# Linear attention with a mixture of experts on one core: q and k loaded as long contiguous runs into a wider tile, with three unit buffers in place of four

## The chip, the cores and the metric

The kernel runs on 1 core of one Trainium2 chip. The metric is the device time of one execution in microseconds (us); lower is better. Before the change three runs took 681.4, 684.25 and 685.61 us, median 684.25.

## What is computed

The reference, cut to what matters. Inputs q, k and v have shape (8, 8, 576, 64): batch, heads, sequence, head size d. All is float32.

```python
def phi(x):
    proj = np.einsum('bhsd,df->bhsf', x, w_phi)          # w_phi: 64 x 128
    proj = proj - np.max(np.abs(proj), axis=-1, keepdims=True)
    return np.concatenate([np.exp(proj), np.exp(-proj)], axis=-1)
q_p, k_p = phi(q), phi(k)
kv = np.einsum('bhsf,bhsd->bhfd', k_p, v)
z = np.sum(k_p, axis=2)
num = np.einsum('bhsf,bhfd->bhsd', q_p, kv)
den = np.einsum('bhsf,bhf->bhs', q_p, z)[..., None] + 1e-06
x = num / den                                            # to rows (token, 512)
# tokens with x @ w_skip > 0: out = x + gate * relu(x @ w1[e]) @ w2[e], e = argmax(x @ w_gate)
# all other tokens: out = x
```

## The kernel before, in words

The program has two stages. The first, attention, works in **units**: one unit is four heads of one batch of either k or q, so 16 units of k and 16 of q. The four heads are two pairs (`pr`). The 576 tokens of a head are 32 runs of 18 tokens; one run of 18 tokens of 64 numbers is 4608 contiguous bytes of the input.

- `st_load` (L250) brings a unit into the tile `u.raw` of shape 128 x 2 x 18 x 32. A partition stands for (half of d, head of the pair, run): the lower 64 partitions hold d from 0 to 31, the upper 64 hold d from 32 to 63. It issues four DMAs, one for each pair and half of d, all on SyncE's queue (line L256). The row of one token is cut in two halves, so each piece that a DMA moves is 32 numbers, 128 bytes. The tile has four buffers, shared by k and q in turn.
- `st_t` (L276) turns the loaded rows with VectorE: L289 transposes the last two of the 18 tokens of both pairs (the tail, step i = 0), L291 the first 16 tokens of one pair (steps i = 1 and 3). After the i = 3 transpose a unit's `raw` buffer is free. ScalarE rounds the result to `hi` (L292), and GpSimd or VectorE forms `lo` = x - `hi` (L294). These come from the pool `hl`.
- `st_proj` multiplies `hi` and `lo` by `wph` and `wpl`, the two parts of w_phi (TensorE, L306 to L308), takes the largest absolute value (VectorE, `m`, L312) and subtracts it (VectorE, `u`, L321).
- `st_exp_k` and `st_exp_q` take the exponentials (ScalarE), and for k form the sums `z` (GpSimd, L353). `st_use_k` makes k'v (L388, L395), `st_use_q` q'(kv) (L486), `norm` divides (VectorE, L437 to L449). `post` finds each token's expert and stores the rows.

A loop over steps t runs the stages of all units as a pipeline with the lags `CFG["lag"]`; the q units follow the k units of the same index by six steps, and one unit takes five steps. At a unit's step i = 0 the load of the next unit of its kind is emitted. v is loaded at L265 and L274 (`v` and its tails `vt`), also on SyncE's queue, as are the stores of rows (L503, L505, L564, L566) and of results (L630, L635). Each engine, and SyncE's queue, runs its instructions in the order in which they stand. TensorE's order is the written one from step 8 to step 79; elsewhere, and on all other engines, a scheduler orders them when the program is built. A DMA into a buffer waits on SyncE until the last reader of the buffer's former content has run.

The second stage, the experts, loads weight chunks (`wraw_c`, L184 and L187), splits them in two parts (L188, L189) and runs the two layers in slots of up to 256 tokens.

Of the kernel before, what the change touches and what calls it, by code (L numbers as in the profile page):

```python
# [18 lines left out]
P = 128  # L19
SLOT = 256  # L20
CFG = {'ql': -2, 'q1': 0, 'vtl': 3, 'at': 6, 'cp': 0, 'ini': 'vvpvppvvpvp', 'inz': '', 'lo': {('E', 0): 'pppvpppp', ('E', 1): 'pppppppp'}, 'lod': 'vppvvvpv', 'seq': ('E', 'E', 'C', 'C', 'SC', 'D', 'DS', 'C', 'C', 'D'), 'pre': (2,), 'rows': (1, 2), 'rxg': (0,) * 6, 'lag': (1, 3, 4, 5, 6), 'post': (4, 5, 7), 'hook': (-1, -1, -1), 'man': (8, 79), 'dnow': 0, 'off': 6, 'order': 'EPAZUT', 'direct': (), 'nb': {'K': 1, 'P': 3, 'U': 2, 'O': 2}, 'apools': (('ld', 2), ('hl', 5), ('up', 5), ('zp', 2), ('ep', 7), ('kvp', 6), ('xp', 2)), 'mpools': (('rawp', 1), ('mx', 2), ('mo', 2), ('wseta', 1), ('wsetb', 1))}


@with_exitstack
def kernel(
# [26 lines left out]
    NA1 = NAUG - 1  # L52
    # a row of xrows: the token, its gate, its number
    XW = DM + 2
    EB = B - 3
    NTE = 9 * (EB // 2) + 9
    # slots: full ones, ones of up to 192 tokens, ones of up to 128
    NSD = (NTOK + E * 63) // SLOT
# [22 lines left out]
    nc.scalar.activation(out=warm, in_=warm, func=AF.Exp)  # L81
    # w_phi in the rows of either head of a pair, and which rows are whose
    wsrc = const.tile([P, NF], F32, name="wsrc")
# [22 lines left out]
    iota_p = const.tile([P, P], F32, name="iota_p")  # L106
    # the tails of a quad's v, each pair in its own rows, zeros in the other's
    vts = [const.tile([P, 2, 2, D], F32, name="vt%d" % j) for j in range(2)]
# [14 lines left out]
    pad0 = const.tile([P, 2, 2], I32, name="pad0")  # L123
    # of every slot: the rows to gather and the rows to scatter to
    ft = const.tile([P, NSL, 4], I32, name="ft")
# [84 lines left out]
    def places(g, pad, v):  # L210
        # v is 0 in an empty place, else 1 + the row to gather; what to add so that no row is scattered from an empty one
        nc.vector.tensor_scalar(out=g, in0=v, scalar1=-1.0, scalar2=0.0, op0=ALU.add, op1=ALU.max)
        nc.vector.tensor_scalar(out=pad, in0=v, scalar1=0.0, scalar2=BIG, op0=ALU.is_equal, op1=ALU.mult)

    early = []
    # ------------------------------------------------------------------ attention
    with ExitStack() as actx:
        pools = {}
        for nm, bufs in CFG["apools"]:
            pools[nm] = actx.enter_context(tc.tile_pool(name=nm, bufs=bufs))  # L220
        ld, hl, zp, up, ep, kvp, xp = (pools[nm] for nm in ("ld", "hl", "zp", "up", "ep", "kvp", "xp"))

        # a head is 32 runs of 18 tokens; partition (half of d, head of the pair, run)
        kv_in = {
            "k": k.rearrange("b h s d -> (b h s d)").rearrange("(u r p t c) -> u r p t c", r=2, p=64, t=18, c=D),
            "q": q.rearrange("b h s d -> (b h s d)").rearrange("(u r p t c) -> u r p t c", r=2, p=64, t=18, c=D),
        }
        vv = v.rearrange("b h s d -> (b h s d)").rearrange("(u h p t c) -> u p h t c", h=4, p=32, t=18, c=D)
        outv = out.rearrange("(b p j) m -> b p j m", p=32, j=18)
        # rows of xrows: two batches after each other, then the tails of both  # L230
        xr = xrows.rearrange("(b x) m -> b x m", x=2 * S)
# [19 lines left out]
        def st_load(u):  # L251
            src = kv_in[u.kind]
            u.raw = ld.tile([P, 2, 18, 32], F32, tag="raw", name="raw", bufs=4)
            for pr in range(2):
                for dh in range(2):
                    nc.sync.dma_start(  # L256
                        out=u.raw[dh * 64:dh * 64 + 64, pr],
                        in_=src[u.g, pr][:, :, dh * 32:dh * 32 + 32],
                    )

# [15 lines left out]
        def st_t(u, i):  # L276
            if i == 0:
                n, sfx = P, "t"
                src = u.raw[:, :, 16:18, :].rearrange("p r t c -> p r (t c)")
            elif i in (1, 3):  # L280
                n, sfx = 4 * P, ""
                src = u.raw[:, i // 2, 0:16, :].rearrange("p (q g) c -> p q g c", g=4)
            else:
                return
            xT = hl.tile([P, n], F32, tag="xT" + sfx, name="xT" + sfx, bufs=2)
            hi = hl.tile([P, n], F32R, tag="hi" + sfx, name="hi" + sfx)
            lo = hl.tile([P, n], F32R, tag="lo" + sfx, name="lo" + sfx)
            if i == 0:
                nc.vector.transpose(out=xT.rearrange("p (r c) -> p r c", r=2), in_=src)  # L289
            else:  # L290
                nc.vector.transpose(out=xT.rearrange("p (g q c) -> p q g c", g=4, q=4), in_=src)  # L291
            nc.scalar.activation(out=hi, in_=xT, func=AF.Copy)  # L292
            nlo[0] += 1
            (nc.vector if CFG["ini"][nlo[0] - 1:nlo[0]] == "v" else nc.gpsimd).tensor_tensor(  # L294
                out=lo, in0=xT, in1=hi.bitcast(F32), op=ALU.subtract)
            u.hlp[(i + 1) // 2] = (hi, lo)
# [136 lines left out]
        def norm(o, xdst, ldst, shape):  # L433
            # o: [P, 4, NAUG]
            den = small.tile([P, 4], F32, tag="den", name="den")
# [16 lines left out]
        def st_use_q(u, i):  # L452
# [5 lines left out]
            if i == 0:  # L458
                # the tails of two batches side by side
                for h in range(4):  # L460
# [52 lines left out]
        def post(b):  # L513
# [40 lines left out]
            )  # L554
            # the gate goes with the token's row
            nc.vector.tensor_reduce(out=ss[:, 0:nt], in_=ex[:, 0:nt], axis=AX.X, op=ALU.add)
# [20 lines left out]
            def rank():  # L577
                # rank of each computed token among those of its expert
                r = bank("O")[:, 0:nt * E]
# [66 lines left out]
        def pick(j):  # L646
            # the expert with the most tokens so far: its first tokens make a slot of their own, done early;
            # the ranks of its later tokens start anew
            cn = bank("O")[:, 0:E]
# [105 lines left out]

    # ------------------------------------------------------------------ experts
    pools = {}
# [31 lines left out]
    def hidden_c(hv):  # L789
        # 192 tokens: the last 64 with both their parts next to each other  # L790
        hh = mo.tile([P, 2, SLOT], F32R, tag="hh", name="hh", bufs=5)
# [8 lines left out]
    def half1(ws, xs):  # L800
        # a slot of 128 tokens: the tokens' columns stay, the weights stream
        _, xh, xl, _, _ = xs
# [38 lines left out]
    def store_c(y, xs):  # L841
        xg, to = xs[0], xs[3]
        # the sums of the high and of the low parts of 64 tokens lie in either half of y
        g, x, r = xg[1][:, DM:DM + 1], xg[1][:, 0:DM], slice(0, 64)
# [10 lines left out]
    def mm1(ws, xs, hooks=()):  # L855
# [3 lines left out]
        for c, (wh, wl) in enumerate(ws):  # L859
            if n < SLOT:  # L860
                # fewer than 256 columns take as long as 256: the products with both parts of x side by side
                hsum = mo.tile([P, 2, n], F32, tag="hsum", name="hsum")
# [65 lines left out]

    # the slots of the tokens that are left: per expert full ones of 256, a rest of up to 192 or of up to 128 in
    # one of its own kind  # L930
    eid = const.tile([1, NSL], I32, name="eid")
# [4 lines left out]
    def tables():  # L936
# [23 lines left out]
        nc.vector.tensor_tensor(out=exc, in0=inc, in1=nn, op=ALU.subtract)  # L960
        # a token's column: its rank, in groups of 128, plus cf[0] where it is below cf[1], else plus cf[2]
        nc.vector.tensor_scalar(out=cf[:, 0], in0=exc[:, 0], scalar1=2.0, scalar2=1.0, op0=ALU.mult, op1=ALU.add)
# [6 lines left out]
        nc.vector.tensor_tensor(out=cf[:, 2], in0=cf[:, 2], in1=cf[:, 1], op=ALU.subtract)  # L969
        # the experts of the slots, and how many there are  # L970
        le = const.tile([1, NSL, E], F32, name="le")
# [6 lines left out]
        nc.vector.tensor_scalar(out=eid[:, 0:NSL], in0=ef, scalar1=float(E - 1), scalar2=None, op0=ALU.min)  # L978
        # the column of each token
        rk = const.tile([P, NT], F32, name="rk")  # L980
# [44 lines left out]
        places(ft[:, NS2:NSL, 0:1], ft[:, NS2:NSL, 2:3], ix[:, 2 * NS2:NCOL].rearrange("p (t s) -> p t s", s=1))  # L1025
        # the slots that the sequence below leaves
        ov = const.tile([1, 8], F32, name="ov")
# [6 lines left out]
        for c, to, left in ((0, 0, "DC"), (1, 3, "CS")):  # L1034
# [100 lines left out]
```

## Time and profile before

| what | value |
|---|---|
| runs | 681.4, 684.25, 685.61 us |
| profiled execution, its own time | 681.4 us |
| span of the profiled execution | 681.4 us |
| TensorE (PE) busy | 600.5 us, 88% |
| VectorE (DVE) busy | 539.6 us, 79% |
| GpSimd (POOL) busy | 440.7 us, 65% |
| ScalarE (ACT) busy | 373.7 us, 55% |
| DMA packets | 221684, of them 160293 under 512 B; 108.17 MB |
| raw loads | 64 for k and 64 for q, 144 KB each |
| mean granted TensorE clock | 0.974 |

A row of the chain or of a group names engine, line and operation, then what it writes `<-` what it reads. "x64" is a count. In rows of waits, the engine at the left stood idle until the one at the right had finished; the numbers are the total in us, the count and the longest. In rows of windows come, for each stretch of the span, the busy time of each engine with its number of instructions, the granted TensorE clock, the busy share of the 16 DMA engines and the rate that they moved. SPq is the queue of SyncE: a row there is the time that it takes to issue DMAs.

### The profile page before, as it was taken

How to read it: one execution, taken by the hardware profiler on the slowest of the kernel's cores; microseconds unless marked ns; L12 is line 12 of the kernel's file. 1: busy time of each engine (PE TensorE's matmuls, PEld its weight loads, DVE VectorE, ACT ScalarE, POOL GpSimd, SP SyncE). 2: the span in 40 equal slices, each digit the busy share in tenths (PEclk: the TensorE clock that was granted, in tenths of full speed). 3: DMA queues.
4: the chain of work that ended last, by engine and by line, in shares of the span. 5: the costliest groups of instructions: out<-in, count | busy, mean ns of one | idle time of the engine just before them, and what ended most of it. 6: DMA issues, size and time to landing. Idle time of an engine off the chain costs nothing. (4 is left out here: it accounts for less than half of the span.)

```text
span 681.4 us, 16258 instructions
## 1 busy us (share of the span) xinstructions
PE 600.5 (88%) x6045; PEld 514.2 (75%) x6045; DVE 539.6 (79%) x1216; ACT 373.7 (55%) x747; POOL 440.7 (65%) x383
## 2 busy tenths in 40 slices
PE   4897999979998889999899991999999989979994
PEld 3585888768877778877788881888878879868893
DVE  6868888887978978978998799679988876677830
ACT  4566665647565475656564533147757556555510
POOL 6886777777777596868774458276575485374411
PEclk9898999999999999999999996899989999999998
DMA  9898664857675667655316387269788877774500
GB/s 130 127 145 157 112 168 91 160 108 133 144 144 90 146 117 133 142 103 114 105 33 195 114 222 232 72 203 296 249 262 268 268 238 267 251 238 139 192 17 27
DMA packets 221684, 108.17 MB, mean 159 GB/s; under 512 B 160293, under 2 KB 202405, under 8 KB 221604
## 3 DMA queue, kind: packets, MB, share of 16 engines
q1 hardware_dynamic: 218272, 97.60, 58.8%
q0 software_dynamic: 3200, 9.45, 4.0%
q8 instruction: 49, 0.80, 0.5%
q14 instruction: 31, 0.25, 0.1%
q10 hardware_dynamic: 132, 0.07, 0.0%
HBM read 83.86 MB, written 24.02 MB: 158 GB/s over the span
## 5 line engine op out<-in xcount | busy, mean ns | idle before, releaser
L189 POOL TENSOR_TENSOR w<-wraw_c,w 128x1024 fp32r<-128x1024 f32 x45 | 109.9, 2454 | 70.6 <-ACT w L188 64.3
L188 ACT ACTIVATE w<-wraw_c 128x1024 fp32r<-128x1024 f32 x96 | 101.0, 1057 | 56.9 <-DMA wraw_c<-in_moe_w_dram 44.9
L353 POOL TENSOR_TENSOR z<-ek 128x512 f32<-128x512 f32 x64 | 81.7, 1277 | 54.9 <-ACT ek L345 45.1
L312 DVE TENSOR_REDUCE m<-ps_P 128x4 f32<-128x512 f32 (+1 forms) x160 | 96.4, 620 | 3.7 <-PE ps_P L308 3.6
L321 DVE TENSOR_TENSOR u<-ps_P,m 128x512 f32<-128x512 f32 (+1 forms) x160 | 95.9, 621 | 0.4
L306 PE MATMUL ps_P<-wph,hi 128*128 128x256 f32 x256 | 80.8, 316 | 16.6 <-ACT hi L292 8.5
L486 PEld LDWEIGHTS ps_O<-kva,eq 128*64 128x64 f32 x2048 | 75.2, 137 | 18.0 <-ACT eqt L373 7.3
L189 DVE TENSOR_TENSOR w<-wraw_c,w 128x1024 fp32r<-128x1024 f32 x51 | 75.4, 1481 | 14.6 <-ACT w L188 14.5
L486 PE MATMUL ps_O<-kva,eq 128*64 128x74 f32 x2048 | 78.4, 229 | 5.0 <-ACT eqt L373 3.2
L294 POOL TENSOR_TENSOR lo<-xT,hi 128x512 fp32r<-128x512 f32 x61 | 78.1, 1280 | 5.0 <-ACT hi L292 4.8
L308 PE MATMUL ps_P<-wph,lo 128*128 128x256 f32 x256 | 73.4, 287 | 0.0
L307 PE MATMUL ps_P<-wpl,hi 128*128 128x256 f32 x256 | 73.2, 286 | 0.0
L388 PE MATMUL ps_K<-ek,v 128*64 128x256 f32 x512 | 71.3, 396 | 1.5 <-DMA v<-in_v_dram 1.5
L372 ACT ACTIVATE eq<-ps_U 128x512 f32<-128x512 f32 x64 | 37.9, 593 | 57.2 <-PE ps_U L366 49.2
L306 PEld LDWEIGHTS ps_P<-wph,hi 128*128 128x128 f32 x256 | 49.4, 193 | 20.4 <-ACT hi L292 9.0
L908 PE MATMUL ps_O<-w,hh 128*128 128x512 f32 x160 | 62.4, 400 | 1.4 <-DVE hh L796 1.3
L836 POOL DMA_INDIRECT out_dram<-o,si x17 | 22.2, 1305 | 54.1 <-DVE o L834 44.4
L913 PE MATMUL ps_O<-w,hlo 128*128 128x512 f32 x120 | 49.0, 410 | 5.1 <-DVE hlo L796 5.1
L307 PEld LDWEIGHTS ps_P<-wpl,hi 128*128 128x128 f32 x256 | 49.7, 194 | 0.0
L308 PEld LDWEIGHTS ps_P<-wph,lo 128*128 128x128 f32 x256 | 49.6, 194 | 0.2 <-DVE lo L294 0.2
L366 PE MATMUL ps_U<-ident,u 128*128 128x128 f32 x288 | 48.4, 286 | 0.6 <-DVE u L321 0.6
L289 DVE STREAM_TRANSPOSE xTt<-raw 128x128 f32<-128x128 f32 x32 | 9.9, 309 | 48.8 <-DMA raw<-in_k_dram 26.8
(233 smaller groups left out, 1570.9 us busy)
## 6 DMA issues: line engine op xcount, KB each, us to landing
wraw_c<-in_moe_w_dram SPq DMA_DIRECT2D x96, 512.0 KB, 4.6
raw<-in_k_dram SPq DMA_DIRECT2D x64, 144.0 KB, 4.0
raw<-in_q_dram SPq DMA_DIRECT2D x64, 144.0 KB, 4.1
v<-in_v_dram SPq DMA_DIRECT2D x64, 128.0 KB, 3.7
out_dram<-xm SPq DMA_DIRECT2D x32, 256.0 KB, 4.4
xrows<-xm SPq DMA_DIRECT2D x8, 516.0 KB, 4.2
xrows<-xm SPq DMA_DIRECT2D x8, 512.0 KB, 4.7
vt<-in_v_dram SPq DMA_DIRECT2D x64, 16.0 KB, 2.6
```

The costliest lines, as they stand in the source:

```text
L188: nc.scalar.activation(out=hi, in_=raw, func=AF.Copy)
L189: (eng or nc.vector).tensor_tensor(out=lo, in0=raw, in1=hi.bitcast(F32), op=ALU.subtract)
L294: (nc.vector if CFG["ini"][nlo[0] - 1:nlo[0]] == "v" else nc.gpsimd).tensor_tensor(out=lo, in0=xT, in1=hi.bitcast(F32), op=ALU.subtract)
L306: nc.tensor.matmul(o, hi[:, c], wph, start=True, stop=False)
L307: nc.tensor.matmul(o, hi[:, c], wpl, start=False, stop=False)
L308: nc.tensor.matmul(o, lo[:, c], wph, start=False, stop=True)
L312: nc.vector.tensor_reduce(out=m[:, 0:nt], in_=pv, axis=AX.X, op=ALU.max, apply_absolute_value=True)
L321: nc.vector.tensor_tensor(out=uu[:, 0:nt, :], in0=pv, in1=m[:, 0:nt].rearrange("p (t o) -> p t o", o=1).broadcast_to([P, nt, NF]), op=ALU. ...
L353: zeng.tensor_tensor(out=z, in0=e[:, 0:2, :], in1=e[:, 2:4, :], op=ALU.add)
L388: nc.tensor.matmul(o[hd * 64:hd * 64 + 64, :], u.v[:, 2 * pr + hd, g * D:(g + 1) * D], u.e[i][:, 2 * j + hd, :], start=(g == 0), stop=False,)
L486: nc.tensor.matmul(ov[s * 64:s * 64 + 64, 2 * j + hd, :], e[:, half, j, hd, s * 64:s * 64 + 64], kva[:, half, 2 * pr + hd, :], start=(half ...
L908: nc.tensor.matmul(y[sub], hh[:, t], wh[:, fi, :], start=first, stop=False)
```

## The change

`st_load` issues two DMAs for a unit in place of four, one for each half of d. Each takes, for every run of 18 tokens, 4480 contiguous bytes (1120 numbers): the run without its last 32 numbers. For the upper half of d it starts 128 bytes later. So in either half of the partitions the numbers that are wanted stand at the first 32 places of each 64, and the other 32 of each token are loaded and not read. The tile is 128 x 2 x 18 x 64, twice as large, and has three buffers. `st_t` reads the first 32 places of each token. The pool `hl` has four buffers of `hi` and `lo` in place of five. Comments are gone; nothing else differs in the source.

```diff
-CFG = {..., 'apools': (('ld', 2), ('hl', 5), ...
+CFG = {..., 'apools': (('ld', 2), ('hl', 4), ...
...
         def st_load(u):
-            src = kv_in[u.kind]
-            u.raw = ld.tile([P, 2, 18, 32], F32, tag="raw", name="raw", bufs=4)
-            for pr in range(2):
-                for dh in range(2):
-                    nc.sync.dma_start(
-                        out=u.raw[dh * 64:dh * 64 + 64, pr],
-                        in_=src[u.g, pr][:, :, dh * 32:dh * 32 + 32],
-                    )
+            x = q if u.kind == "q" else k
+            u.raw = ld.tile([P, 2, 18, D], F32, tag="raw", name="raw", bufs=3)
+            for r, run, n, dh in [(dh * 64, 0, 64, dh) for dh in range(2)]:
+                nc.sync.dma_start(
+                    out=u.raw[r:r + n].rearrange("p r t c -> p r (t c)")[:, :, 0:RUN - HD],
+                    in_=bass.AP(
+                        tensor=x.tensor, offset=x.offset + (u.g * 128 + run) * RUN + dh * HD,
+                        ap=[[RUN, n], [64 * RUN, 2], [1, RUN - HD]]))
...
         def st_t(u, i):
             if i == 0:
                 n, sfx = P, "t"
-                src = u.raw[:, :, 16:18, :].rearrange("p r t c -> p r (t c)")
+                src = u.raw[:, :, 16:18, 0:HD]
             elif i in (1, 3):
                 n, sfx = 4 * P, ""
-                src = u.raw[:, i // 2, 0:16, :].rearrange("p (q g) c -> p q g c", g=4)
+                src = u.raw[:, i // 2, 0:16, 0:HD].rearrange("p (q g) c -> p q g c", g=4)
...
             if i == 0:
-                nc.vector.transpose(out=xT.rearrange("p (r c) -> p r c", r=2), in_=src)
+                nc.vector.transpose(out=xT.rearrange("p (r t c) -> p r t c", r=2, t=2), in_=src)
```

`RUN` is 18 * 64 numbers and `HD` is 32. The change also makes the scheduler order VectorE, ScalarE, GpSimd and SyncE anew; TensorE's order differs only in its first 50 rows.

The first place is SyncE's queue in the middle of the attention stage, up to the stores of one batch (`out_dram`, `xrows`). `vt_90` and `vt_91` are the two buffers for the tails of v. Before, the v loads stand between a k load (`raw<-in_k_dram`) and a q load:

```order
L256 DMA raw<-in_k_dram 64x18x32 x4
L265 DMA v<-in_v_dram 32x4x256 x4
L274 DMA vt_90<-in_v_dram 32x2x64 x2
L256 DMA raw<-in_q_dram 64x18x32 x4
L630 DMA out_dram<-xm 32x4x512 x4
L274 DMA vt_91<-in_v_dram 32x2x64 x2
L564 DMA xrows<-xm 512x1x258
L566 DMA xrows<-xt 128x258
```

After it, the q load and the k load that follows stand next to each other, behind the v loads:

```order
L265 DMA v<-in_v_dram 32x4x256 x4
L274 DMA vt_90<-in_v_dram 32x2x64 x2
L255 DMA raw<-in_q_dram 64x2x1120 x2
L255 DMA raw<-in_k_dram 64x2x1120 x2
L630 DMA out_dram<-xm 32x4x512 x4
L274 DMA vt_91<-in_v_dram 32x2x64 x2
L564 DMA xrows<-xm 512x1x258
L566 DMA xrows<-xt 128x258
```

What moved: the k load went from ahead of the v loads to right behind the q load, and eight issues for two units became four.

The second place is VectorE, from the transpose that frees a `raw` buffer (the first row) to the first transpose that reads the load which was waiting for that buffer (the last row). Before, at the k unit of index 10:

```order
L291 STREAM_TRANSPOSE xT<-raw 128x4x4x32
L312 TENSOR_REDUCE m<-ps_P 128x4
L312 TENSOR_REDUCE m<-ps_P 128x2
L321 TENSOR_TENSOR u<-ps_P,m 128x512
L321 TENSOR_TENSOR u<-ps_P,m 128x256
L437 TENSOR_SCALAR den<-ps_O 128x4
L441 RECIPROCAL rec<-den 128x4
L448 TENSOR_TENSOR xm<-ps_O,rec 128x2x128
L449 TENSOR_TENSOR lgm<-ps_O,rec 128x2x18
L312 TENSOR_REDUCE m<-ps_P 128x4 x2
L321 TENSOR_TENSOR u<-ps_P,m 128x512
L289 STREAM_TRANSPOSE xTt<-raw 128x128
```

After it, at the q unit of index 9:

```order
L291 STREAM_TRANSPOSE xT<-raw 128x4x4x32
L321 TENSOR_TENSOR u<-ps_P,m 128x512
L437 TENSOR_SCALAR den<-ps_O 128x4
L291 STREAM_TRANSPOSE xT<-raw 128x4x4x32
L441 RECIPROCAL rec<-den 128x4
L312 TENSOR_REDUCE m<-ps_P 128x4
L448 TENSOR_TENSOR xm<-ps_O,rec 128x2x128
L449 TENSOR_TENSOR lgm<-ps_O,rec 128x2x18
L312 TENSOR_REDUCE m<-ps_P 128x4
L321 TENSOR_TENSOR u<-ps_P,m 128x512 x2
L289 STREAM_TRANSPOSE xTt<-raw 128x128
```

What moved: at this place two transposes that free buffers now stand three rows apart, the first for the q load and the second for the k load. From the freeing transpose to the first use VectorE has 15 to 24 instructions before (15, 16, 24 and 17 over four successive units), counting the first use; after the change it is 12, 20 or 18, 15 and 18.

More of the change, by code (lines that the diff above doesn't have):

```diff
@@ L20 @@
 SLOT = 256
-CFG = {'ql': -2, 'q1': 0, 'vtl': 3, 'at': 6, 'cp': 0, 'ini': 'vvpvppvvpvp', 'inz': '', 'lo': {('E', 0): 'pppvpppp', ('E', 1): 'pppppppp'}, 'lod': 'vppvvvpv', 'seq': ('E', 'E', 'C', 'C', 'SC', 'D', 'DS', 'C', 'C', 'D'), 'pre': (2,), 'rows': (1, 2), 'rxg': (0,) * 6, 'lag': (1, 3, 4, 5, 6), 'post': (4, 5, 7), 'hook': (-1, -1, -1), 'man': (8, 79), 'dnow': 0, 'off': 6, 'order': 'EPAZUT', 'direct': (), 'nb': {'K': 1, 'P': 3, 'U': 2, 'O': 2}, 'apools': (('ld', 2), ('hl', 5), ('up', 5), ('zp', 2), ('ep', 7), ('kvp', 6), ('xp', 2)), 'mpools': (('rawp', 1), ('mx', 2), ('mo', 2), ('wseta', 1), ('wsetb', 1))}
+CFG = {'ql': -2, 'q1': 0, 'vtl': 3, 'at': 6, 'cp': 0, 'ini': 'vvpvppvvpvp', 'inz': '', 'lo': {('E', 0): 'pppvpppp', ('E', 1): 'pppppppp'}, 'lod': 'vppvvvpv', 'seq': ('E', 'E', 'C', 'C', 'SC', 'D', 'DS', 'C', 'C', 'D'), 'pre': (2,), 'rows': (1, 2), 'rxg': (0,) * 6, 'lag': (1, 3, 4, 5, 6), 'post': (4, 5, 7), 'hook': (-1, -1, -1), 'man': (8, 79), 'dnow': 0, 'off': 6, 'order': 'EPAZUT', 'direct': (), 'nb': {'K': 1, 'P': 3, 'U': 2, 'O': 2}, 'apools': (('ld', 2), ('hl', 4), ('up', 5), ('zp', 2), ('ep', 7), ('kvp', 6), ('xp', 2)), 'mpools': (('rawp', 1), ('mx', 2), ('mo', 2), ('wseta', 1), ('wsetb', 1))}
 @with_exitstack
@@ L221 @@
         ld, hl, zp, up, ep, kvp, xp = (pools[nm] for nm in ("ld", "hl", "zp", "up", "ep", "kvp", "xp"))
[L224 to L227, printed above, removed]
+        RUN = 18 * D
+        HD = D // 2
         vv = v.rearrange("b h s d -> (b h s d)").rearrange("(u h p t c) -> u p h t c", h=4, p=32, t=18, c=D)
```

## The prediction

> **What bounds the kernel now.** I read the table of windows first, to separate the stages, then the waits of VectorE and TensorE in the stage that the change touches. All loads of `raw` lie in the attention stage, so the question is what ends last there. In these rows of windows come the busy times of PE, PEld, DVE, ACT and POOL, then TensorE's granted clock, the DMA engines' share and their rate.
>
> ```profile
> 17.00:340.00 323.00, 294.17 (x3753) 245.06 (x3752) 269.48 (x738) 196.62 (x465) 247.55 (x236) 0.99 0.66 129
> 340.00:357.00 17.00, 17.00 (x214) 14.03 (x214) 15.64 (x51) 11.64 (x24) 13.57 (x12) 1.00 0.11 33
> 17.00:51.00 34.00, 30.63 (x296) 23.63 (x294) 24.80 (x49) 20.75 (x48) 29.70 (x28) 0.95 0.92 136
> 442.00:510.00 68.00, 64.37 (x369) 56.16 (x369) 60.35 (x73) 40.73 (x64) 46.10 (x26) 0.97 0.81 250
> ```
>
> From 17 to 340 us TensorE is busy 294.2 of 323 us: idle 28.8 us. VectorE is idle 53.5 us. From 340 to 357, where no `raw` is loaded any more (the last q load is issued at 305.4, below), TensorE has no idle time at all. So the same pipeline can fill TensorE, and something between 17 and 340 keeps it from doing so. The waits in that stretch (total in us, count, longest):
>
> ```profile
> DVE xTt L289 <- DMA raw<-in_k_dram: 26.2, 13, 4.0
> DVE xTt L289 <- DMA raw<-in_q_dram: 18.2, 12, 3.4
> ...
> DVE xT L291 <- DMA raw<-in_q_dram: 0.8, 1, 0.8
> DVE m L312 <- PE ps_P L308: 0.8, 3, 0.3
> ...
> PE ps_P L306 <- DVE u L321: 12.3, 12, 3.8
> PE ps_O L619 <- POOL rhs L608: 7.5, 6, 1.6
> PE ps_O L486 <- ACT eqt L373: 3.2, 4, 1.1
> ...
> ACT hi L292 <- PE ps_P L307: 0.6, 1, 0.6
> ```
>
> VectorE waits for almost nothing but `raw`: 26.2 + 18.2 + 0.8 = 45.2 us. Its order is fixed, so while it stands before L289 for a load, the `m` and `u` behind it stand too, and TensorE then waits for a bank that `u` has not read (12.3 us). The `rhs` and `eqt` waits are ends of chains that also pass through VectorE. 45.2 us of waits on VectorE go with 28.8 us of idle TensorE: 0.64 us for each us.
>
> Why do the loads come late? The timeline of VectorE shows two of them, and SyncE's queue the issues:
>
> ```profile
> 162.31 0.70 DVE L291 STREAM_TRANSPOSE xT<-raw 128x512 f32<-128x512 f32 x1
> 162.94 0.98 DVE L312 TENSOR_REDUCE m<-ps_P 128x4 f32<-128x512 f32 x2
> 163.84 1.00 DVE L321 TENSOR_TENSOR u<-ps_P,m 128x512 f32<-128x512 f32 x2
> 164.77 0.14 DVE L437 TENSOR_SCALAR den<-ps_O 128x4 f32<-128x4 f32 x1
> 164.95 0.18 DVE L441 RECIPROCAL rec<-den 128x4 f32<-128x4 f32 x1
> 165.16 0.42 DVE L448 TENSOR_TENSOR xm<-ps_O,rec 128x256 f32<-128x256 f32 x1
> 165.50 0.19 DVE L449 TENSOR_TENSOR lgm<-ps_O,rec 128x36 f32<-128x36 f32 x1
> 165.61 1.28 DVE L312 TENSOR_REDUCE m<-ps_P 128x4 f32<-128x512 f32 x2
> 166.80 0.68 DVE L321 TENSOR_TENSOR u<-ps_P,m 128x512 f32<-128x512 f32 x1
> 169.44 0.31 DVE L289 STREAM_TRANSPOSE xTt<-raw 128x128 f32<-128x128 f32 x1 [1.96 <-DMA raw<-in_k_dram]
> ...
> 140.48 0.70 DVE L291 STREAM_TRANSPOSE xT<-raw 128x512 f32<-128x512 f32 x1
> ...
> 148.79 0.31 DVE L289 STREAM_TRANSPOSE xTt<-raw 128x128 f32<-128x128 f32 x1 [2.39 <-DMA raw<-in_k_dram]
> ...
> 163.04 3.10 SPq L256 DMA_DIRECT2D raw<-in_k_dram  x4
> ```
>
> L291 ends at 163.01, and SyncE issues the load that waited for that buffer at 163.04. Its data is there at 169.44, 6.4 us later. VectorE had 4.5 us of other work (163.01 to 167.48) and waited 1.96. At 140.48 it was 7.6 us against a cover of 5.2. So a wait is **the load's time L minus the cover**, the work that VectorE has between the transpose that frees the buffer and the first use. The cover is 4.5 to 6.2 us, L 6.4 to 7.6.
>
> **The change, part by part.** The load's time first:
>
> ```profile
> L256 SPq DMA_DIRECT2D raw<-in_k_dram x64: 539/764/2527, 0.8 to 281.2; - x64
> ...
> L256 SPq DMA_DIRECT2D raw<-in_q_dram x64: 539/747/2112, 11.9 to 305.4; - x64
> L184 SPq DMA_DIRECT2D wraw_c<-in_moe_w_dram x48: 372/373/1907, 366.1 to 628.3; - x48
> ...
> wraw_c<-in_moe_w_dram SPq DMA_DIRECT2D x96, 512.0 KB, 4.6
> ...
> vt<-in_v_dram SPq DMA_DIRECT2D x64, 16.0 KB, 2.6
> ...
> q0 software_dynamic: 3200, 9.45, 4.0%
> ```
>
> Before, a unit is 4 x 147,456 B = 589,824 B in 128 B pieces. The row of 17 to 51, full of these, moves 136 GB/s at a share of 0.92: 148 GB/s if full. That is 4.0 us of data. The smallest load (`vt`, 16 KB) lands 2.6 us after its issue, nearly all of it fixed. 2.6 + 4.0 = 6.6 us, inside the measured 6.4 to 7.6, so this way of counting holds.
>
> After, a unit is 2 x 64 x 2 x 4480 B = 1,146,880 B in long runs: nearly twice the bytes. Their rate is not in the trace. The row of 442 to 510, with weight loads, gives 250 / 0.81 = 309 GB/s. The largest packets are those of queue q0: 9.45 MB in 4.0% of 16 engines for 681.4 us, which is 347 GB/s at a mean of 2953 B. Bounds: below, 148 GB/s, as if length did not matter (7.7 us of data, L = 10.3); above, 347 GB/s and a shorter fixed part (L about 5). I take 330 GB/s, between the two rows nearest in size: 3.5 us, **L = 6.1 us**. The second issue, 0.37 us by the weight loads' row, lies under the first one's data.
>
> The Trainium skill ("DMA: Bandwidth & Descriptors", section "Why small descriptors are slow (HBM only)") gives a packet about 3 bus cycles beside one for each 32 B. By that, 128 B packets run at 4/7 of peak and 4480 B ones at 140/143, so the unit's data would take 13% longer after than before, not 12% less. The trace speaks against so small a penalty: 148 GB/s is under half of 309, which itself comes with packets of 1 to 2 KB. It stays as a rival.
>
> Next the cover. The order after the change shows ten instructions between the freeing L291 and the q load's L289. By the starts in the rows above (L312 and L321 0.60 each, L291 0.63, L437 0.18, L441 0.21, L448 0.34, L449 0.10) they are 5 x 0.60 + 0.63 + 0.18 + 0.21 + 0.34 + 0.10 = 4.5 us. The same addition over the other places gives 6.4, 6.0 and 5.2 to 6.1 us, where before it gives 4.5, 6.2, 5.2 and 5.1. So the third buffer's loss costs hardly any cover; the scheduler has moved the transposes that free buffers forward.
>
> The k load now stands right behind the q load on SyncE, so its data queues behind 3.5 us of q's. At the place shown, the k buffer is freed 1.9 us after q's (0.63 + 0.60 + 0.18 + 0.5). Its data is there 2 x 3.5 + 2.6 = 9.6 us after q's release; VectorE reaches it at 1.9 + 6.4 + the q wait of 1.6 = 9.9. It is covered. Per four units the waits are 1.6, 0, 0.1 and about 0.3: 2 us. For 28 units in the steady part that is 14 us, and I add 4 for the first few, whose order is another: **18 us in place of 45**. 27 us less, at 0.64, is 17 us off TensorE's idle time.
>
> Other edits. Transposes now read every second group of 32 numbers. Their 64 + 32 instructions move as much as before:
>
> ```profile
> L291 DVE STREAM_TRANSPOSE xT<-raw x64: 665/701/712, 7.1 to 342.2; 128x512 f32<-128x512 f32 x64
> ...
> L289 DVE STREAM_TRANSPOSE xTt<-raw x32: 264/311/316, 9.1 to 309.7; 128x128 f32<-128x128 f32 x32
> ...
> PE ps_K L388 <- DMA v<-in_v_dram: 1.5, 1, 1.5
> ```
>
> L289 already reads two separate pieces and pays for its 128 numbers no more than L291's slope, so I take nothing; if the gaps doubled L291 it would be 64 x 0.7 = 45 us, which I keep in the slow case. Four buffers of `hi` in place of five: 64 tiles in 335 us are one every 5.2 us, so a buffer is written again after 21 us in place of 26; ScalarE waited once, 0.6 us, for TensorE there. Nothing. SyncE issues 64 DMAs less (4 x 0.75 - 2 x 0.37 = 2.2 us less for each unit); only the first v, behind eight issues of `raw`, can gain by that, at most the 1.5 us that TensorE waited for it. The first transposes now need both loads of a unit (0.8 + 2.6 + 3.5 = 6.9 us, where L291 began at 7.1). Together 0, within 1.5. The expert stage keeps its order and shifts.
>
> Sum: 681.4 - 17 = **664.4 us** against the profiled execution, whose time is its span. The median of the runs shown, 684.25, is 2.85 above it, so I say 667.
>
> **Rivals.**
> - *The load's time does not shrink* (the skill's rule, or a rate near 250 GB/s because v loads and stores share the engines). At 250 GB/s a unit's data takes 4.6 us and L is 7.2. The q waits are 7.2 - 4.5 = 2.7 and 1.2, the k loads behind them (9.2 + 2.6 = 11.8 us after q's release) wait 0.8 and 1.0: 5.7 for four units, 44 us with the first ones. That is the 45 of before: 684 us, no change. For it: the window's own rate is 250. Against it: its share is 0.81, not 1.
> - *Slower: two units in one burst.* The same mechanism below 250 GB/s, which is the point from which it decides. With 2.29 MB back to back at 200 GB/s, midway to the row of 148, a unit takes 5.7 us: waits of 3.8, 1.9, 2.3 and 2.1, 10.1 for four units, 77 us in all. 32 more than before at 0.64 is 20 us: 704. For it: three buffers leave no other slack. Against it: 0.66 is the share in the stage, and bursts of weight loads land in 4.6 us.
> - *All of TensorE's idle time goes.* If L is 5 us the waits nearly vanish and TensorE fills as from 340 to 357: 28.8 us, 655. Against it: `rhs` and `eqt` waits (10.7 us) have links outside VectorE.
>
> **How the numbers follow.** 0.55 for the forecast, 0.2 for no change, 0.14 for slower, 0.11 for the full gain. A difference under 1% (6.8 us) is about what a measurement of this kernel cannot tell from none. The forecast's own range is 657 to 676, from L of 5.5 to 6.6. With the full gain below it and the no-change case above, and part of the slower one, 653 to 690 leaves out less than 2 in 10. Faster by over 1%: 0.55 + 0.11 = 0.66; within: 0.20; slower: 0.14.
>
> **What would show it.** In the new profile: L289's waits for `raw` near 18 us in place of 45, mostly at q loads; landing of `raw` near 5 to 6 us from issue; under 20,000 packets below 512 B (160293 now, of them 32 x 4608 for `raw`); TensorE idle near 12 us in the same stage; the last q load some 15 us earlier. L289 waiting 45 us or more in total, or TensorE idle as before with VectorE waiting elsewhere (for `lo`, or for TensorE), would make the prediction wrong; so would L291 well above 0.70 us.

## The result, and the profile after

The changed kernel takes **739.35 us** (median of 4 runs, 733.47 to 742.94), against 684.93 us for the kernel before on the same chip: a ratio of 1.078, 95% interval 1.072 to 1.085. It is slower by 54 us, where 667 us was predicted. All ratios leave out executions in a slower state: one of the four with short stalls (1462.08 us), one of the ten with three buffers and the old loads, and the one of the alternate-partition kernel that was profiled (1.7% above its fastest).

The first two views are the rows of the tile `raw` (count: shortest/median/longest ns, first and last start) and the page's DMA issues (KB each, median us from issue to landing), after the change:

```profile
L291 DVE STREAM_TRANSPOSE xT<-raw x64: 660/699/712, 9.7 to 402.6; 128x512 f32<-128x512 f32 x64
L255 SPq DMA_DIRECT2D raw<-in_k_dram x32: 595/605/1772, 0.8 to 342.4; - x32
L255 SPq DMA_DIRECT2D raw<-in_q_dram x32: 596/607/1316, 9.7 to 372.4; - x32
```
```profile
raw<-in_k_dram SPq DMA_DIRECT2D x32, 560.0 KB, 10.0
raw<-in_q_dram SPq DMA_DIRECT2D x32, 560.0 KB, 7.5
...
out_dram<-xm SPq DMA_DIRECT2D x32, 256.0 KB, 8.8
```

The transposes cost what they did (699 ns against 701), though they now skip every second group. But the last L291 starts at 402.6 us where it was 342.2: all of the loss, 60.4 us, lies in the attention stage. (From there to the end it is 739.3 - 402.6 = 336.7 us, against 339.2 before.) A raw load lands 7.5 to 10 us after its issue (4.0 and 4.1 us for the smaller loads before), and the stores of `xm` take 8.8 us (4.4 before).

The next view is the table of windows: the first row is of before, from its first matmul to its last L291, the others of after. Columns as in the prediction: PE, PEld, DVE, ACT, POOL busy, granted clock, DMA share, GB/s.

```profile
8.50:342.20 333.70, 303.20 (x3801) 252.51 (x3803) 278.23 (x757) 203.20 (x479) 253.54 (x240) 0.99 0.67 129
```
```profile
17.70:402.60 384.90, 330.45 (x3850) 271.47 (x3851) 277.72 (x762) 209.84 (x484) 256.24 (x242) 0.91 0.63 151
...
17.00:51.00 34.00, 23.61 (x136) 17.84 (x137) 26.02 (x48) 18.32 (x41) 24.32 (x23) 0.82 0.98 197
```

Three things stand here. The stage starts at 17.7 us in place of 8.5: **9.2 us**. TensorE is idle for 384.90 - 330.45 = 54.5 us in place of 30.5: **24 us**. And TensorE's busy time is 330.5 us in place of 303.2 for nearly the same matmuls (3850 against 3801 in the rows; 1.3% are 4 us): **27 us**, with a mean granted clock of 0.91 in place of 0.99. 9 + 24 + 27 = 60. The last row gives the rate: with the DMA engines full (0.98), the loads, those of v among them, move 197 GB/s, where the prediction took 330.

The waits of VectorE and of TensorE from 17 to 400 us after the change:

```profile
DVE xTt L289 <- DMA raw<-in_q_dram: 43.6, 14, 4.7
DVE xTt L289 <- DMA raw<-in_k_dram: 32.2, 13, 3.6
DVE den L437 <- PE ps_O L486: 15.8, 13, 2.7
```
```profile
PE ps_P L306 <- DVE u L321: 41.7, 18, 4.5
```

VectorE waits 75.8 us for raw (45.2 before), and TensorE 41.7 us for `u`, which stands behind L289 (12.3 before). One such wait, on VectorE and on SyncE's queue:

```profile
121.88 0.70 DVE L291 STREAM_TRANSPOSE xT<-raw 128x512 f32<-128x512 f32 x1
...
130.90 0.31 DVE L289 STREAM_TRANSPOSE xTt<-raw 128x128 f32<-128x128 f32 x1 [4.05 <-DMA raw<-in_q_dram]
...
136.15 0.31 DVE L289 STREAM_TRANSPOSE xTt<-raw 128x128 f32<-128x128 f32 x1 [2.21 <-DMA raw<-in_k_dram]
```
```profile
122.60 1.26 SPq L255 DMA_DIRECT2D raw<-in_q_dram  x2
```

From the freeing L291's end (122.58) to the first use it is 8.3 us, forecast at 6.1. The cover is 8.32 - 4.05 = 4.3 us, forecast at 4.5. (The k load behind it, forecast as covered, waits 2.21.) So the wait is still load time minus cover, as predicted, and the load time is what went wrong.

### The profile page after: what moved, and what is told of

Read it like the earlier page. It is cut to its first block, busy times and chain, and to the rows that moved or that the text cites. A ratio compares the mean times of both kernels' runs of the same rounds, so it can differ in the third digit from the quotient of the medians.

```text
span 739.3 us, 16191 instructions
## 1 busy us (share of the span) xinstructions
PE 626.7 (85%) x6045; PEld 531.7 (72%) x6045; DVE 540.2 (73%) x1216; ACT 378.6 (51%) x747; POOL 443.0 (60%) x383
## 2 busy tenths in 40 slices
DMA packets 81396, 125.99 MB, mean 170 GB/s; under 512 B 11813, under 2 KB 53925, under 8 KB 81316
## 5 line engine op out<-in xcount | busy, mean ns | idle before, releaser
L189 POOL TENSOR_TENSOR w<-wraw_c,w 128x1024 fp32r<-128x1024 f32 x45 | 108.0, 2418 | 66.6 <-ACT w L188 60.4
L486 PEld LDWEIGHTS ps_O<-kva,eq 128*64 128x64 f32 x2048 | 80.8, 146 | 14.7 <-issue 9.1
L189 DVE TENSOR_TENSOR w<-wraw_c,w 128x1024 fp32r<-128x1024 f32 x51 | 78.5, 1542 | 12.8 <-ACT w L188 12.8
L306 PEld LDWEIGHTS ps_P<-wph,hi 128*128 128x128 f32 x256 | 51.3, 201 | 48.7 <-issue 25.6
L486 PE MATMUL ps_O<-kva,eq 128*64 128x74 f32 x2048 | 83.6, 238 | 0.3 <-DVE lgt L449 0.3
L388 PE MATMUL ps_K<-ek,v 128*64 128x256 f32 x512 | 80.3, 436 | 0.1
L308 PE MATMUL ps_P<-wph,lo 128*128 128x256 f32 x256 | 75.2, 295 | 0.0
L307 PE MATMUL ps_P<-wpl,hi 128*128 128x256 f32 x256 | 75.2, 294 | 0.0
L289 DVE STREAM_TRANSPOSE xTt<-raw 128x128 f32<-128x128 f32 x32 | 9.9, 309 | 76.0 <-DMA raw<-in_q_dram 43.6
L307 PEld LDWEIGHTS ps_P<-wpl,hi 128*128 128x128 f32 x256 | 51.8, 202 | 0.0
L344 ACT ACTIVATE ek<-u 128x512 f32<-128x512 f32 x64 | 40.3, 630 | 22.2 <-DVE u L321 22.1
```

The costliest lines, as they stand in the source:

```text
L189: (eng or nc.vector).tensor_tensor(out=lo, in0=raw, in1=hi.bitcast(F32), op=ALU.subtract)
L306: nc.tensor.matmul(o, hi[:, c], wph, start=True, stop=False)
L307: nc.tensor.matmul(o, hi[:, c], wpl, start=False, stop=False)
L308: nc.tensor.matmul(o, lo[:, c], wph, start=False, stop=True)
L388: nc.tensor.matmul(o[hd * 64:hd * 64 + 64, :], u.v[:, 2 * pr + hd, g * D:(g + 1) * D], u.e[i][:, 2 * j + hd, :], start=(g == 0), stop=False,)
L486: nc.tensor.matmul(ov[s * 64:s * 64 + 64, 2 * j + hd, :], e[:, half, j, hd, s * 64:s * 64 + 64], kva[:, half, 2 * pr + hd, :], start=(half ...
```

## Experiments on the rate

How long one packet takes can be read from the DMA queue's row: packets, MB, and their time as a share of 16 engines' time. From 125 to 131 us after the change there is little but raw:

```profile
DMA packets 334, 1.36 MB, mean 226 GB/s; under 512 B 32, under 2 KB 32, under 8 KB 333
...
q1 hardware_dynamic: 333, 1.35, 103.3%
```

1.033 x 16 x 6 us = 99 us for some 301 packets of 4480 B: **329 ns** each, 13.6 GB/s for each engine. Two theories: A, the receiving side (each load goes to 64 neighbouring partitions only); B, the runs themselves (their length, or how they are read from DRAM).

**One load to all 128 partitions.**

```
-for r, run, n, dh in [(dh * 64, 0, 64, dh) for dh in range(2)]: ...
-    out=raw[r:r + n] ..., in_=AP(..., ap=[[RUN, n], [64 * RUN, 2], [1, RUN - HD]])
+for r2 in range(2): ...
+    out=raw[:, r2] ..., in_=AP(..., ap=[[HD, 2], [RUN, 64], [1, RUN - HD]])
```

> The changed kernel with its two loads cut the other way: one load for each pair of heads, to all 128 partitions (64 of the lower half of d, then 64 of the upper half), in place of one for each half of d to 64 partitions. Bytes (1,146,880 for a unit), number of loads (two), packets (4480 B each), buffers and sizes stay as in the changed kernel. Theory A (a load that goes to 64 partitions runs at half the rate): a packet takes 160 to 190 ns where it took 328, the rate while the DMA engines are full is above 300 GB/s where it was 200, VectorE and ScalarE wait under 60 us for raw where they waited 136 together, and the time falls to 670 to 700 us. Theory B (runs of 4480 B are slow wherever they go, by their length, by their start 128 B into a run, or because twice the bytes are moved): a packet still takes about 330 ns, and the time stays at 733 to 745 us.

It took 1265.95 us, ratio 1.848 (1.838 to 1.858). Neither theory had that. The queue and the window, 132 to 140 us, with nothing but raw in flight:

```profile
q1 hardware_dynamic: 96, 0.43, 13.0%
```
```profile
132.00:140.00 8.00, 0.00 (x0) 0.00 (x0) 0.00 (x0) 0.00 (x0) 0.00 (x0) 0.50 0.13 54
```

The share is 0.13, about 2 of 16: the load's outermost step on the DRAM side has only two values, and no more engines than that worked. Each packet took 0.13 x 16 x 8 / 96 = **173 ns**, 26 GB/s for each engine. So a 4480 B packet is not slow by its length; in the changed kernel, with all 16 engines at work on one half, it takes 329 ns. That the outermost steps set how many engines a load gets is also what the Trainium skill states ("DMA: Bandwidth & Descriptors", section "Why a DMA increments its semaphore by 16 and not by 1"); the share of 0.13 agrees.

**Runs cut into pieces.**

```
-    out=raw[r:r + n] [:, :, 0:RUN - HD], in_=AP(..., ap=[[RUN, n], [64 * RUN, 2], [1, RUN - HD]])
+    out=raw[r:r + n] ... "p r (w x) -> p r w x", w=4, in_=AP(..., ap=[..., [64 * RUN, 2], [280, 4], [1, 280]])
```

> The changed kernel with each run of 4480 B asked for as four pieces of 1120 B, to the same 64 partitions by the same two loads; the order of the instructions on every engine is the same. Theory A (64 partitions): the rate stays at 200 GB/s, a 1120 B packet takes 80 ns or more, and the time is 733 to 750 us. Theory B in its form 'packets above 4 KB are slow': the rate rises to that of the weight loads (309 GB/s in packets of 1 to 2 KB), and the time falls to 665 to 700 us.

739.88 us, ratio 1.082 (1.076 to 1.088). But it tells nothing of length: its page counts 81396 packets, as many as the changed kernel's, so the four adjoining pieces went as one. It is a second measurement of the changed kernel. Its L291 row shows how far two traces of one kernel differ:

```profile
L291 DVE STREAM_TRANSPOSE xT<-raw x64: 665/700/712, 9.9 to 396.7; 128x512 f32<-128x512 f32 x64
```

The stage ends at 396.7 us here and at 402.6 above, so the end of a stage, read from one trace, is good to some 6 us.

**Two queues.**

```
-    nc.sync.dma_start(
+    (nc.sync, nc.scalar)[dh].dma_start(
```

> The changed kernel with the load of the lower half of d on SyncE's queue and that of the upper half on ScalarE's, so that both are in flight together; bytes, packets and partitions of each load as in the changed kernel. Theory A in its form 'each group of 64 partitions takes at most about 210 GB/s': together they move above 300 GB/s, and the time falls to 670 to 710 us, with some loss because ScalarE spends 0.6 us on each of 32 issues and waits there for buffers. Theory B (the engines themselves take 330 ns for such a run): 200 GB/s in all, 735 to 760 us.

739.27 us, ratio 1.081 (1.075 to 1.087). At one place the halves were issued 0.3 us apart (99.27 on SyncE, 99.57 on ScalarE), yet their data moved one after the other. The queues' rows, from 100.5 to 102.5 and from 103 to 105.5 us:

```profile
q1 hardware_dynamic: 108, 0.48, 93.9%
```
```profile
q10 hardware_dynamic: 118, 0.53, 99.8%
```

So it goes in most bursts of this run, and its time cannot tell A from B. But where both halves were issued at the same moment (127.47 us), their packets did share the engines. The totals and queues from 129 to 136 us:

```profile
DMA packets 482, 2.01 MB, mean 287 GB/s; under 512 B 36, under 2 KB 37, under 8 KB 481
...
q1 hardware_dynamic: 260, 1.07, 51.9%
q10 hardware_dynamic: 221, 0.92, 47.1%
```

The same loads, to the same rows, move 287 GB/s in the first seven us of a burst with both halves in flight. In the changed kernel it is 227 in the first seven (124 to 131). That speaks for A.

**Alternate partitions.** The reading side stays; only the receiving partitions change.

```
-    out=raw[r:r + n] ...
+    out=raw[dh::2] ...
```

> The changed kernel with one number changed on the receiving side of each load: the 64 runs of the lower half of d go to partitions 0, 2, 4, ... 126 and those of the upper half to 1, 3, 5, ... 127, in place of 0 to 63 and 64 to 127. What is read from DRAM, the 64 partitions of each load, the packets, their number and order, the buffers and the instructions stay; the heads are computed on mixed-up rows. Theory A, now in the form 'neighbouring halves of the partitions share a path of about 215 GB/s, whatever reads from DRAM': a packet takes 170 to 190 ns, a full stretch moves above 320 GB/s, VectorE waits under 30 us for raw, and the time is 655 to 690 us. Theory B (the reading side is slow: runs of 4480 B at steps of 4608 B read by 16 engines at once) and theory A in its plain form (any 64 partitions): packets stay at 330 to 345 ns and the time at 733 to 745 us.

The queue from 111.5 to 114 us and from 111 to 117, VectorE's waits from 17 to 351 us, L291's row and the window that ends with it:

```profile
DMA packets 233, 0.95 MB, mean 381 GB/s; under 512 B 21, under 2 KB 21, under 8 KB 232
...
q1 hardware_dynamic: 232, 0.95, 99.6%
```
```profile
DMA packets 457, 1.87 MB, mean 311 GB/s; under 512 B 44, under 2 KB 44, under 8 KB 455
...
q1 hardware_dynamic: 455, 1.84, 93.1%
```
```profile
DVE xTt L289 <- DMA raw<-in_k_dram: 26.4, 12, 4.5
DVE xTt L289 <- DMA raw<-in_q_dram: 10.0, 7, 2.5
```
```profile
L291 DVE STREAM_TRANSPOSE xT<-raw x64: 666/700/715, 7.9 to 351.3; 128x512 f32<-128x512 f32 x64
```
```profile
13.00:351.30 338.30, 309.00 (x3850) 256.68 (x3851) 280.56 (x765) 209.51 (x486) 255.73 (x242) 0.98 0.55 173
```

The rate is 381 GB/s in 2.5 us near the start of a burst, where a packet takes about 0.996 x 16 x 2.5 / 211 = 189 ns. Over six us, as in the changed kernel's row, it is 311 GB/s at a share of 0.93, or 334 if full, and a packet takes 0.931 x 16 x 6 / 411 = 217 ns; there it was 226 GB/s and 329 ns. **Theory A in its second form holds**: what limits the changed kernel's loads is that each goes to neighbouring partitions of one half. Not the count of 64, the packets, or the reading from DRAM, which are all the same here. The attention stage ends at 351.3 us in place of 402.6, so, by these two traces, the low rate and what follows from it cost about 51 of the 60 us.

The whole kernel took 976.13 us, ratio 1.427 (1.417 to 1.438), and missed its 655 to 690: mixed-up rows send the tokens to other experts (VectorE is busy 622 us in place of 540), so its time behind the attention stage says nothing on the change. But 351.3 is later than before's 342.2 all the same: **at about the rate that was forecast, this trace shows no gain.** (Nor is a loss shown: 9 us is little beside the 6 us between two traces above.)

**Alternate loads**, with every row where it belongs:

```
-for r, run, n, dh in [(dh * 64, 0, 64, dh) for dh in range(2)]:
+for r, run, n, dh in [(dh * 64 + h * 32, h * 32, 32, dh) for h in range(2) for dh in range(2)]:
```

> The changed kernel with each unit's two loads cut into four of 32 runs each, issued in turn to partitions 0 to 31, 64 to 95, 32 to 63 and 96 to 127; everything lands where the changed kernel has it. It asks whether the rate of the run with mixed-up rows can be had with the rows where they belong, by letting neighbouring loads go to different halves. If the DMA engines get far enough apart to work on both halves at once: full stretches above 260 GB/s, waits of VectorE for raw under 60 us, 690 to 720 us. If they stay in step (theory A, each load by itself at about 215 GB/s): packets stay near 340 ns and the time at 733 to 750 us, since SyncE issues two more loads for each unit.

718.67 us, ratio 1.050 (1.046 to 1.054): over a third of the loss is back. Its L291 row, VectorE's waits from 17 to 390 us, and the queue from 117.5 to 123.5:

```profile
L291 DVE STREAM_TRANSPOSE xT<-raw x64: 667/700/712, 12.0 to 380.7; 128x512 f32<-128x512 f32 x64
```
```profile
DVE xTt L289 <- DMA raw<-in_q_dram: 33.7, 13, 4.8
DVE xTt L289 <- DMA raw<-in_k_dram: 19.3, 8, 3.8
DVE xTt L289 <- DMA vt<-in_v_dram: 11.4, 4, 3.0
```

```profile
DMA packets 404, 1.47 MB, mean 245 GB/s; under 512 B 77, under 2 KB 77, under 8 KB 403
...
q1 hardware_dynamic: 403, 1.46, 100.3%
```

53 us of waits in place of 76; 11.4 us more of L289's waits are put down to `vt`, which L289 does not read, so the waits for raw may be 64 us. The time is that of the first forecast. The rate of a full stretch, 245 GB/s, is not: it lies between 226 and the 260 that I had set. That loads which take turns between the halves are quicker fits theory A; how far the engines get apart was not measured.

## Experiments on buffers, start and stalls

**Buffers alone**, with the loads of before.

```
-u.raw = ld.tile([P, 2, 18, 32], F32, tag="raw", name="raw", bufs=4)      ('hl', 5)
+u.raw = ld.tile([P, 2, 18, 32], F32, tag="raw", name="raw", bufs=3)      ('hl', 4)
```

> The kernel before, with its loads of 128 B pieces, but with three buffers for raw in place of four and four for hi and lo in place of five. It tells what the buffers alone cost. Theory A and the prediction's step (the scheduler moves the transposes forward, so the cover stays near 5 us): 681 to 692 us, VectorE's waits for raw 45 to 60 us. Rival C (the third buffer's loss is a large part of the slowdown, since a load can start only one unit ahead): VectorE's waits for raw above 80 us and 705 to 730 us.

685.91 us, ratio 1.002 (0.999 to 1.005). As the prediction said, three buffers in place of four cost nothing, with these loads. VectorE's waits for raw from 17 to 340 us are even shorter, 21.4 + 15.0 + 0.8 = 37.2 us (45 to 60 was expected, 45.2 before), and the time is none the better for it.

```
-u.raw = ... bufs=4)      ('hl', 5)
+u.raw = ... bufs=6)      ('hl', 4)
-if i == 0 and s // 5 + 1 < len(us): st_load(us[s // 5 + 1])
+if s == 0: st_load(us[1])
+if i == 0 and s // 5 + 2 < len(us): st_load(us[s // 5 + 2])
```

> The kernel before, with its 128 B pieces, but with six buffers for raw in place of four (four for hi and lo in place of five) and each stream's load started two units ahead in place of one. It tests the prediction's relation 'VectorE's waits for raw cost 0.64 us of TensorE each' from the other side, with the rate of the loads left alone. If it holds: VectorE waits under 12 us for raw in place of 45, and the time falls by 20 to 29 us to 655 to 665. Rival: the loads only collide more with v and the stores, or VectorE waits elsewhere: 680 to 690 us.

675.04 us, ratio 0.991 (0.988 to 0.994): a gain of 6 us, under 1%, not of 20 to 29. Then the same six buffers with the loads started as before:

> The kernel before with six buffers for raw (four for hi and lo), but each load started one unit ahead as before. It tells which half of the earlier run with six buffers gave its gain of 0.9%: the buffers or the earlier start. If it is the buffer that a load waits for: VectorE's waits for raw under 20 us, 673 to 677 us. If the order on SyncE's queue holds the loads back: waits 35 to 45 us, 680 to 685 us.

**672.40 us**, ratio 0.986 (0.981 to 0.991): the shortest time here, by a gain that is still under 2%. Its only edit is the first pair of lines above. The buffers give the gain, the earlier start nothing more. VectorE's waits from 17 to 340 us, and the window from the first matmul to the last L291:

```profile
DVE xTt L289 <- DMA raw<-in_k_dram: 10.1, 4, 4.4
DVE xT L291 <- POOL lo L294: 9.0, 12, 1.5
DVE m L312 <- PE ps_P L308: 8.3, 10, 2.3
DVE den L437 <- PE ps_O L486: 6.5, 12, 0.7
DVE xTt L289 <- DMA raw<-in_q_dram: 3.5, 6, 1.1
```
```profile
8.50:335.10 326.60, 307.42 (x3850) 256.16 (x3851) 279.18 (x765) 205.21 (x484) 254.46 (x242) 0.98 0.68 131
```

The waits for raw fall from 45 to 14 us, but VectorE now waits 24 us for `lo`, `m` and `den`, where it waited 0.8 us for `m`. TensorE's idle time falls from 30.5 to 19.2 us: 0.36 us for each us of raw wait, where the prediction had 0.64. (The stage is 7 us shorter; I have not traced the rest of the gain.)

**The start.** After the change, ScalarE's `wph` (L95) waits 11 us for `w_phi`, whose data shares the DMA engines with the raw loads, and TensorE begins 9.2 us later.

```
 for dh in range(2):
-    nc.scalar.dma_start(out=wsrc[dh * 64:dh * 64 + 64], ...)
+    nc.sync.dma_start(out=wsrc[dh * 64:dh * 64 + 64], ...)
```

> The changed kernel with the two loads of w_phi on SyncE's queue ahead of the first raw loads, in place of ScalarE's queue beside them. If the late start (first matmul at 17.8 us against 8.5) comes from w_phi's data standing behind the raw loads on the DMA engines: ScalarE's wait for w_phi shrinks from 11 to under 4 us, the first matmul comes at 11 to 13 us, and the time falls by 4 to 7 us, to 731 to 737. If it comes from the first k load itself: first matmul still after 16 us and no change.

TensorE's first matmul, and the window that follows:

```profile
12.56 0.58 PE L306 MATMUL ps_P<-wph,hi 128*128 128x256 f32 x1 [12.56 <-ACT hi L292]
```
```profile
17.00:51.00 34.00, 23.66 (x123) 17.39 (x124) 23.09 (x44) 17.32 (x38) 23.07 (x22) 0.81 0.99 200
```

The reason was right: it begins 5.2 us earlier. But 737.66 us, ratio 1.082 (1.076 to 1.088), misses the forecast of 731 to 737 and is not told apart from the changed kernel; that the stage ends 1.1 us earlier (401.5) says nothing beside the 6 us between two traces. The next stretch takes the 5 us back: with the DMA engines full, TensorE runs 123 matmuls from 17 to 51 us after the 15 that it now runs ahead of 17 us; the changed kernel ran 136 in all. So no cost of the late start by itself, beside the rate, is seen; one of some 3 us could hide in the noise.

**Stalls without any change of the loads.** A useless VectorE instruction ahead of L289:

```
 xT = hl.tile([P, n], F32, tag="xT" + sfx, ...)
+if i == 0 and u.g % 2 == 1:          # short: every unit, 4 x 512
+    nc.vector.tensor_reduce(out=xT[:, 0:8], in_=stl (8 x 512), axis=AX.X, op=ALU.max)
```

> The kernel before, with its loads and four buffers, plus one useless VectorE instruction of about 4.8 us (a reduction of 8 x 512 numbers) ahead of L289 in every second unit: 16 x 4.8 = 77 us of VectorE time, as much as VectorE waited for raw in the changed kernel (76), in stretches as long as its longest waits (4.7). No load is changed. Theory D (what the changed kernel pays is VectorE standing still, and TensorE's clock halves after each idle gap of 2 us or more that follows from it): time 715 to 740 us, at least eight stretches of half clock in the attention stage where before has two, TensorE's busy time 10 us or more above before's for the same matmuls. Rival E (the clock falls for another reason, such as the DMA traffic): two or three stretches of half clock, busy time as before, at most 712 us.

> The same 77 us of useless VectorE work, in pieces of 2.4 us ahead of L289 in every unit (32 x 2.4). Theory D: VectorE's work in the stage grows from 269 to 346 us where the stage took 323, so the stage takes 30 us more, but TensorE's gaps stay shorter and the clock falls less often than with the long pieces: 705 to 718 us, and below the run with long pieces. Rival E: the same time as with the long pieces.

They took 755.98 us, ratio 1.109 (1.103 to 1.116), and 746.44 us (median of three), ratio 1.091 (1.083 to 1.099). The added rows, long and short, with their busy us and mean ns (the instruction stands at line 291 of these kernels), and the windows of the attention stage, long and short:

```profile
L291 DVE TENSOR_REDUCE xTt<-stl 128x8 f32<-128x4096 f32 x16 | 70.2, 4386 | 0.0
L291 DVE TENSOR_REDUCE xTt<-stl 128x4 f32<-128x2048 f32 x32 | 72.6, 2272 | 5.5 <-POOL lot L300 5.4
```
```profile
9.00:412.30 403.30, 325.46 (x3801) 267.85 (x3803) 344.45 (x772) 206.77 (x479) 253.37 (x240) 0.89 0.56 106
```
```profile
9.00:403.40 394.40, 317.77 (x3800) 263.13 (x3801) 345.25 (x788) 207.02 (x479) 253.82 (x240) 0.94 0.57 109
```

About 70 us of VectorE time make the stage 61 to 70 us longer (333.7 before): at this place a us added to VectorE costs 0.84 to 1 us, though a us of wait taken away gave back a third. Both times lie above their forecasts (715 to 740 and 705 to 718); for the short pieces I had expected half of that cost. The clock part held. TensorE is idle about as long in both (77.8 and 76.6 us), for the same number of matmuls as in before's row, and yet busy 325.5 us at a clock of 0.89 with long stalls, 317.8 at 0.94 with short ones, 303.2 at 0.99 without. The DMA engines moved less than before (106 and 109 GB/s against 129). So rival E is out: stalls alone bring the clock down, and long ones more.

## Why the prediction was wrong, step by step

- **Wait = load time minus cover**: right for the q load at the place shown, with a cover of 4.3 us for a forecast of 4.5.
- **Rate 330 GB/s, so L = 6.1**: this step failed. 197 to 226 GB/s when full, and L = 8.3 us. I took the rate from the weight loads and from queue q0, by the size of their packets. No row there was a load of long runs to 64 neighbouring partitions, and the alternate-partition run shows that this is what counts: 311 to 381 GB/s at the same sizes. There L is 6.1 us, from the end of the freeing L291 (109.27) to L289's start, as forecast:

```profile
108.57 0.70 DVE L291 STREAM_TRANSPOSE xT<-raw 128x512 f32<-128x512 f32 x1
...
115.42 0.31 DVE L289 STREAM_TRANSPOSE xTt<-raw 128x128 f32<-128x128 f32 x1 [2.02 <-DMA raw<-in_q_dram]
```

- **The rule I overlooked.** The Trainium skill ("SBUF — State Buffer", section "Door 1: The DMA port swizzle (why `[64,N]` ≈ `[32,N]`)") states that partitions 0 to 63 reach only 8 of 16 ports, about 218 GB/s. The traces agree: 197 to 226 GB/s in long runs (the 226 at a share of 1.03), 311 to 381 when a load's partitions alternate over both halves. Only the start of a burst is faster: 300 GB/s from 124.6 to 125.6 us. The loads of before, at 148 GB/s, lay below that limit and did not show it.
- **The slower rival** had the mechanism and the threshold (below 250 GB/s), though not why the rate is low, at a chance of 0.14. Its 704 us at 200 GB/s had 77 us of waits, measured 75.8, but priced 32 us more of them at 0.64, 20 us.
- **0.64 us of TensorE for each us of VectorE's wait**: failed both ways. Taking away 31 us of waits gave 0.36 each, as other waits took their place; adding VectorE time cost 0.84 to 1 each. An average over one trace is not the price of the next us.
- **The clock**: in no term of the sum. With the row's 0.91, TensorE ran at half clock for (1 - 0.91) x 2 x 384.9 = 69 us of the stage, against 7 us before, and its busy time grew by 27 us, of which 4 go with the greater number of rows. (This takes the clock to be either full or half, as in the windows at the end.)
- **18 us of waits at the assumed rate**: also failed; 36.4 us in the alternate-partition run, whose rate is about the assumed one. The forecast had the k loads nearly covered, but they waited 26.4 us. The three longest of these waits, 4.0 to 4.5 us, are for loads with `out_dram` stores right behind them on the queue; that the stores take the engines from the loads was not tested. TensorE's first matmul there is at 14.41 us, so that it was then idle 351.3 - 14.4 - 309.0 = 27.9 us, where before it was 30.5. That is 2.6 us less, not 17: by this trace the forecast of 667 fails even with its rate.
- **Second issue at 0.37 us**: 0.605 measured; it lies under the first load's data, as said.
- **The start at 0, within 1.5**: TensorE began 9.2 us later, since I followed k's own data and not `w_phi` on the other queue. The run with `w_phi` first shows no gain from putting this right.
- **Transposes, four buffers of `hi`, three of `raw` at 0**: right (699 ns; 685.91 us, ratio 1.002). For the transposes the argument was weak: 311 ns for 128 numbers and 701 for 512 cannot part a fixed cost from a price of the gaps.

## What to carry to other kernels

Price a load by where it goes as well as by its packets: read the rate from a row whose loads go to the same partitions, and where none exists, let the range reach down to the lowest full rate. Do not convert waits into time by the mean of one trace; look at what is late next, since a wait taken away may give a third and one added may cost all of it. When loads are late for lack of buffers and not of rate, more buffers of the old load (here six, 1.4% shorter) are the cheaper thing to try.

## What the runs showed of the hardware

- Loads of 4480 B runs to 64 neighbouring partitions moved 226 GB/s over six us at a full share; to every second partition it was 311 over six us at a share of 0.93. With two engines at work a packet took 173 ns, with sixteen on one half 329, with sixteen and alternating partitions 189 to 217.
- TensorE's granted clock falls to half after a short idle gap. The windows after the change, around one gap of 3.7 us:

```profile
105.40:109.20 3.80, 0.14 (x2) 0.11 (x1) 2.53 (x11) 1.28 (x5) 2.94 (x4) 0.76 0.72 266
109.20:114.00 4.80, 4.80 (x46) 3.67 (x47) 4.03 (x12) 1.77 (x5) 2.54 (x3) 0.50 0.36 118
114.00:138.00 24.00, 22.61 (x311) 19.33 (x312) 16.07 (x50) 14.29 (x33) 17.62 (x19) 1.00 0.66 155
```

  46 matmuls in 4.8 us at a clock of 0.50 (9.6 in a us), then 311 in 24 us at 1.00 (13 in a us). Over the whole stage 24 us more of idle time went with 27 us more of busy time, and with the added stalls 46 to 47 us went with 15 to 22: idle time of TensorE costs more than itself. The Trainium skill ("TensorE: Matmul & The Clock Gate", section "What's actually happening") puts the fall after an idle window of about 3.4 us; here the clock is already below 1 inside a gap of 3.7 us (0.76 in its row), and after a gap of 2.35 us (from 138.46 to 140.81) it was 0.50 from 141.8 to 144.8.
- An outermost step of two on the DRAM side left 14 of 16 DMA engines idle (share 0.13), at nearly twice the kernel's time.
- Two loads issued 0.3 us apart on two queues moved their data one after the other; two that were issued at the same moment shared the engines.
